# Keys times values in 64x64 quadrants with two permuting products, in a linear attention followed by a highway layer

## The chip, the core and the metric

The kernel runs on one core of a Trainium2 chip. The core has five engines that run side by side, each with its own queue of instructions: TensorE (PE, matrix products; its weight loads are listed apart as PEld), VectorE (DVE), ScalarE (ACT), GpSimd (POOL) and SyncE (SP, which here only issues transfers). Sixteen transfer engines (DMA) move data between the main memory and the on-chip memory. Products land in a separate accumulator memory, PSUM. The metric is the device time of one execution in microseconds (us).

## What is computed

Eight batches, eight heads, 576 tokens, 64 dims a head. Each head's queries go through a softmax over their dims, its keys through a softmax over the tokens; the keys and values of a head make a 64x64 matrix, and the queries are multiplied with it. The result, 4608 tokens by 512, goes through a highway layer with two 512x512 weights.

```python
def _attn_ref(q, k, v):                       # (8, 8, 576, 64) each
    q_s = np.exp(q - np.max(q, axis=-1, keepdims=True))
    q_s = q_s / (np.sum(q_s, axis=-1, keepdims=True) + 1e-09)
    k_s = np.exp(k - np.max(k, axis=2, keepdims=True))
    k_s = k_s / (np.sum(k_s, axis=2, keepdims=True) + 1e-09)
    kv = np.einsum('bhsd,bhse->bhde', k_s, v)
    return np.einsum('bhsd,bhde->bhse', q_s, kv)

def _moe_ref(x, w_h, w_t, b_t):               # x: (4608, 512)
    H = np.maximum(x @ w_h, 0.0)
    T = 1.0 / (1.0 + np.exp(-(x @ w_t + b_t)))
    return T * H + (1.0 - T) * x
```

## The kernel before

The whole program is a list of steps written out by hand, ORDER (lines 17 to 55). A step such as `kv_3` or `xe_5:A` calls one small function with a batch, group or tile number, and a letter picks the engine where there is a choice (A for ACT, D for DVE, P for POOL). Each engine works off its instructions in the order in which the list issues them; waits between engines follow from the data.

A batch b goes through these steps. `k`, `v` and `q` issue the loads on SP's queue, each buffer threefold. `ek` takes the exponential of the keys on ACT, `vc` casts the values to 16 bits, with a column of ones beside them. `kv` multiplies them on PE: for each head the 576 tokens lie as 9 slices of 64 partitions, and a product of one slice (64 tokens) takes 32 dims of one head, the even or the odd ones, as weights and 65 columns of values as the moving side. That is 8 heads x 9 slices x 2 halves = 144 products of 64x32 per batch, in tile positions (64 hh, 32 g). The 32 partitions of position g hold one half of the dims of a head, the other half lies in the same partitions at another place (m) of the free dimension. `kr` and `kn` on DVE take the reciprocal of the ones column's sums and scale the matrix into `kvb`. `eq` is the exponential of the queries on ACT, and `tr` turns them on DVE, two 16-bit dims as one 32-bit element; that is why the dims come in even and odd ones.

Then come 20 groups of tokens, `xu`, each of two tiles of 128 tokens (every fifth group is one tile, from the rest of two batches): PE multiplies turned queries and `kvb`, the two halves m = 0 and 1 added in PSUM. `kv` and `xu` share one PSUM buffer of four banks (pool ps_x, one buffer), so each waits until the one before has been read. `rs` and `x` on DVE divide by the sum and write x in 16 bits.

For each of 36 tiles: `xt` transposes x on PE, `xe` copies it out of PSUM, `bw` puts the bias in the gate's bank (a product with ones on PE, or a copy by ACT), `mt` and `mh` are the four products each with the two weights, `th` the tanh on ACT, `dd` the maximum on DVE, `gg`, `uu` and `oo` the rest on POOL or DVE, and `st` or `st1` the store. `wtc`, `whd` and `whc` prepare the weights once; `fill` issues idle products on PE at the start.

Lines that the prediction's steps touch: L222 `ek`, L227 `vc`, L243 `kv`, L250 `kr`, L253 `kn`, L260 `eq`, L278 `tr`, L291 and L301 `xu`, L313 `rs`, L319 `x`, L326 `xt`, L332 `xe`, L339 and L341 `bw`, L346 `mt`, L352 `mh`, L359 and L362 `th`, L366 `dd`, L155 `fill`.

Of the kernel before, what the change touches and what calls it, by code (L numbers as in the profile page):

```python
# [19 lines left out]
k_1_0_2 xe_1:D whc_0:A xu_1 whd_2:D whd_3:P whc_2:A mt_1_0 th_1_0 mt_0_0 rs_1 x_1 xt_2 ek_1_0_2 v_1_2_2 xe_2:D  # L20
vc_1_2_2:P mh_0 dd_0 mh_2 th_0_0 gg_0_0:P mh_1 bw_2_0 dd_2 bw_3_0:A gg_1_0:P dd_1 v_1_0_2 k_1_2_2 ek_1_2_2 q_1_0_8
eq_1_0_8 xt_3 xe_3:D mt_2_0 vc_1_0_2:D uu_0_0:P mh_3 q_1_8_10 dd_3 oo_0_0:D mt_3_0 tr_1_0_8 uu_1_0:P oo_1_0:P th_2_0
k_2_0_4 gg_2_0:P kv_1 kr_1 kn_1 eq_1_8_10 tr_1_8_8 v_2_0_4 bw_4_0 th_3_0 uu_2_0:P bw_5_0:A xu_2 rs_2 x_2 xt_4 xu_3
ek_2_0_4 tr_0_16_2 oo_2_0:P gg_3_0:P xe_4:D uu_3_0:P rs_3 tr_1_16_2 x_3 xt_5 mt_4_0 xe_5:A mh_5 q_2_0_18 v_3_0_4
k_3_0_4 th_4_0 vc_2_2_2:D vc_2_0_2:A q_3_0_18 xt_6 oo_3_0:P xu_4 rs_4 gg_4_0:P x_4 q_4_0_18 xe_6:A mt_5_0 mh_4 th_5_0
dd_5 dd_4 xt_8 xe_8:D eq_2_0_8 tr_2_0_8 kv_2 kr_2 kn_2 bw_8_0:A gg_5_0:P mt_8_0 eq_2_8_10 tr_2_8_8 mh_6 bw_6_0:A xt_7
# [20 lines left out]
eq_7_8_10 st_11 kv_7 oo_22_0:D kr_7 kn_7 uu_24_0:P mh_28 dd_23 dd_28 xt_29 mh_26 dd_26 xu_17 rs_17 xe_29:A xt_30
bw_29_0:A mt_29_0 x_17 bw_28_0:A oo_25_0:P mt_28_0 xe_30:A th_29_0 uu_23_0:P oo_24_0:P mh_27 oo_23_0:P st_10 tr_7_8_8
bw_27_0:A uu_26_0:P th_28_0:S uu_28_0:D xt_31 xe_31:A tr_7_16_2 dd_27 mt_27_0 bw_31_0:A th_27_0:S xt_32 xu_18
tr_6_16_2 rs_18 xe_32:A uu_27_0:D gg_29_0:P mt_31_0 x_18 oo_26_0:P th_31_0 mh_29 dd_29 mh_30 bw_30_0:A mt_30_0  # L50
oo_28_0:D bw_32_0:A st_13 oo_27_0:P st_12 uu_29_0:P gg_31_0:P dd_30 th_30_0:S xu_19 rs_19 oo_29_0:P uu_30_0:D
# [8 lines left out]
def kernel(  # L60
# [168 lines left out]
    def kv_of(b):  # L229
        return T[f"kvps{b}"][:, 0:2, 0:130].rearrange("p m (c e) -> p m c e", c=2)  # L230

    def kv(e, b):


# [1 line left out]
        for turn in range(2):
            for c in range(2):
                for j in range(NJ):
                    for g in range(4):
                        h = 4 * c + g  # L240
                        hh, i, m = h % 2, h // 2, (turn + h) % 2
                        rows, cols = slice(64 * hh, 64 * hh + 64), slice(32 * g, 32 * g + 32)
                        nc.tensor.matmul(  # L243
                            ps[cols, m, 65 * c:65 * c + 65], T[f"ek{b}"][rows, j, i, m:D:2],
                            v16[b % NV][rows, i, j, 0:65], start=(j == 0), stop=(j == NJ - 1),
                            skip_group_check=True, tile_position=(64 * hh, 32 * g))
# [34 lines left out]
    def xu(e, u):  # L281
        bs, J, its = groups[u]
        t = T[f"xu{u}"] = ps_x.tile([P, 4, DM], FP32, tag="xu", name=f"xu_{u}")
        if len(bs) == 1:
            for a in range(2):
                for c in range(2):
                    for m in range(2):
                        for g in range(4):
# [2 lines left out]
                            nc.tensor.matmul(  # L291
                                t[:, g, col:col + 65], turned_q(bs[0], c, m, 256 * J + P * a, P)(rows),
                                kvb[bs[0] % NKV][rows, m, c, 0:65], start=(m == 0), stop=(m == 1),
                                skip_group_check=True, tile_position=(32 * g, 0))
            return
        for c in range(2):
            for m in range(2):
                for w, b in enumerate(bs):
                    for g in range(4):
# [103 lines left out]
    def st1(e, i, h=0):  # L403
# [14 lines left out]
        wtc=wt_cast, whc=wh_cast, whd=wh_less_identity, ek=ek, vc=vc, kv=kv, kr=kr, kn=kn, eq=eq, tr=tr,  # L418
# [36 lines left out]
```

## Time and profile before

| | |
|---|---|
| median of 3 runs | 144.22 us (143.59 to 144.29) |
| the profiled execution | 142.23 us, its span 140.5 us |
| PE busy | 112.2 us (80% of the span), 2267 products |
| DVE busy | 98.2 us (70%) |
| ACT busy | 90.9 us (65%) |
| POOL busy | 85.9 us (61%) |
| moved by DMA | 40.17 MB, mean 286 GB/s |
| kv, L243 | 1152 products of 64x32, 12.5 us busy |
| xu, L291 and L301 | 640 products, 9.2 us busy |
| mt and mh, L346 and L352 | 292 products, 78.2 us busy |
| ek, L222 | 10 instructions, 17.4 us busy |

The span is the time from the first to the last instruction of one execution; 1.7 us lie around it. A line of the groups gives line, engine, operation, the program's names of what is written and read, shapes and count, then busy time and the mean of one instruction. Products of PE overlap, so the mean of one (197 ns in kv) is longer than the distance from one to the next. The chain of waits is followed back from the last instruction: at each step to what released it, or to the instruction before it; "issue" is time in which an engine waited for nothing that the profile shows. PEclk and "clock" are the share of full speed that TensorE's clock was granted.

### The profile page before, as it was taken

What the parts mean: (1) busy time and instruction counts of PE and PEld (TensorE: products, weight loads), DVE (VectorE), ACT (ScalarE), POOL (GpSimd) and SP (SyncE); (2) the same over time, 40 slices, a digit from 0 to 9 for tenths busy, and PEclk for the clock granted to TensorE, in tenths of its full rate; (3) what the DMA queues carried; (4) which work ended last, traced back from release to release, by engine and by line L of the source; (5) the groups of instructions that cost most, each with busy time, mean ns of one, the idle gap of its engine ahead of it and who ended that gap; (6) DMA issues with size and microseconds to landing.
All of it is one profiled execution on the core that took longest, in us unless ns stands there. A gap on an engine that the chain in (4) does not pass through costs nothing.

```text
span 140.5 us, 5171 instructions
## 1 busy us (share of the span) xinstructions
PE 112.2 (80%) x2267; PEld 58.9 (42%) x2267; DVE 98.2 (70%) x176; ACT 90.9 (65%) x121; POOL 85.9 (61%) x93
## 2 busy tenths in 40 slices
PE   6947879936997599189923999399999999999930
PEld 2315245524364255035522456145565464544510
DVE  3703786977477597557923498287999999998890
ACT  3345376776577595916931689349999978866710
POOL 0001546999139469494980437903998879989930
PEclk9997899996599999959995599869999999999996
DMA  4999999999999999999999999100291052724362
GB/s 138 261 398 407 401 392 387 394 395 398 392 396 410 394 387 392 403 402 405 396 401 399 404 396 355 40 0 0 82 398 53 5 201 103 296 84 167 132 269 106
DMA packets 14890, 40.17 MB, mean 286 GB/s; under 512 B 914, under 2 KB 1170, under 8 KB 14868
## 3 DMA queue, kind: packets, MB, share of 16 engines
q1 hardware_dynamic: 14576, 39.59, 73.9%
q8 instruction: 17, 0.28, 0.8%
q10 hardware_dynamic: 292, 0.27, 0.6%
q14 instruction: 5, 0.04, 0.1%
HBM read 30.41 MB, written 9.44 MB: 284 GB/s over the span
## 4 chain that ended last, share of the span: by engine, by line
PE 63%; DVE 13%; issue 10%; DMA 6%; ACT 3%; SPq 2%; DVEq 0%
PE tps L346 22%; PE gps L352 21%; PE turned L326 7%; PE kv L243 7%; DMA v<-in_v_dram 6%; PE xu L291 4%; DVE d L366 3%; DVE et L278 3%; DVE x L319 2%; ACT qe L260 2%; DVE o L392 2%; SPq L168 2%; DVE v L227 1%; PE turned L155 1%; DVE xT L332 1%
## 5 line engine op out<-in xcount | busy, mean ns | idle before, releaser
L392 POOL TENSOR_TENSOR o<-u,x 128x512 f32<-128x512 f16 (+1 forms) x30 | 35.6, 1195 | 7.4 <-DVE u L377 6.8
L346 PE MATMUL tps<-w16t,xT 128*128 128x512 f16 (+1 forms) x148 | 39.7, 403 | 0.2 <-DVE xT L332 0.2
L352 PE MATMUL gps<-w16h,xT 128*128 128x512 f16 x144 | 38.5, 400 | 0.0
L380 POOL TENSOR_TENSOR u<-g,d 128x512 f16<-128x512 f16 x23 | 27.7, 1212 | 4.7 <-DVE d L366 4.2
L366 DVE SCALAR_TENSOR_TENSOR d<-x,gps 128x512 f16<-128x512 f16 x36 | 24.3, 679 | 4.8 <-PE gps L352 4.7
L371 POOL TENSOR_SCALAR g<-th 128x512 f16<-128x512 f16 x23 | 14.1, 618 | 20.3 <-ACT th L362 20.3
L260 ACT ACTIVATE qe<-q 128x1024 f16<-128x1024 f32 (+1 forms) x16 | 18.6, 1164 | 6.3 <-DVE kvb L253 1.9
L319 DVE TENSOR_TENSOR x<-xu,rs 128x1024 f16<-128x1024 f32 (+1 forms) x20 | 22.2, 1112 | 0.3
L278 DVE STREAM_TRANSPOSE et<-qe 128x512 f32<-128x512 f32 (+1 forms) x24 | 20.0, 835 | 2.9 <-ACT qe L260 2.9
L243 PE MATMUL kv<-v,ek 64*32 64x65 f16 x1152 | 12.5, 197 | 10.3 <-issue 7.3
L346 PEld LDWEIGHTS <-xT 128*128 128x128 f16 x148 | 14.0, 104 | 15.0 <-issue 3.7
L352 PEld LDWEIGHTS <-xT 128*128 128x128 f16 x144 | 13.8, 102 | 14.7 <-issue 2.8
L222 ACT ACTIVATE ek<-k 128x2304 f16<-128x2304 f32 (+1 forms) x10 | 17.4, 1736 | 3.5 <-DMA k<-in_k_dram 3.5
L339 ACT COPY tps<-ball 128x512 f32<-128x512 f32 x29 | 16.8, 592 | 3.3 <-DVE d L366 3.1
L362 ACT ACTIVATE th<-tps 128x512 f16<-128x512 f32 x23 | 13.6, 596 | 8.1 <-PE tps L346 8.0
L332 ACT COPY xT<-turned 128x512 f16<-128x512 f16 x18 | 10.6, 586 | 12.8 <-PE turned L326 12.8
L326 PE MATMUL turned<-idh,x 128*128 128x128 f16 x144 | 15.0, 231 | 4.0 <-DVE x L319 3.3
L243 PEld LDWEIGHTS <-ek 64*32 64x32 f16 x1152 | 11.0, 94 | 13.1 <-issue 8.2
L326 PEld LDWEIGHTS <-x 128*128 128x128 f16 x144 | 10.6, 102 | 11.1 <-DVE x L319 4.1
L291 PE MATMUL xu<-kvb,et 32*128 32x65 f16 x512 | 7.8, 197 | 6.9 <-issue 5.1
L359 ACT ACTIVATE tps<-tps 128x512 f32<-128x512 f32 (+1 forms) x14 | 7.7, 550 | 5.8 <-PE tps L346 5.5
L291 PEld LDWEIGHTS <-et 32*128 32x128 f16 x512 | 5.5, 97 | 13.6 <-issue 7.3
(42 smaller groups left out, 82.3 us busy)
## 6 DMA issues: line engine op xcount, KB each, us to landing
out_dram<-o SPq DMA_DIRECT2D x16, 512.0 KB, 5.6
k<-in_k_dram SPq DMA_DIRECT2D x6, 1152.0 KB, 14.5
v<-in_v_dram SPq DMA_DIRECT2D x6, 1152.0 KB, 16.1
q<-in_q_dram SPq DMA_DIRECT2D x6, 1152.0 KB, 15.3
k<-in_k_dram SPq DMA_DIRECT2D x4, 576.0 KB, 9.1
q<-in_q_dram SPq DMA_DIRECT2D x2, 640.0 KB, 12.1
v<-in_v_dram SPq DMA_DIRECT2D x4, 288.0 KB, 4.1
v<-in_v_dram SPq DMA_DIRECT2D x2, 576.0 KB, 11.5
```

The source lines that it names most:

```text
L222: nc.scalar.activation(t[:, :, c:c + n].rearrange("p j c d -> p c j d"), src[:, c:c + n], AF.Exp)
L243: nc.tensor.matmul(ps[cols, m, 65 * c:65 * c + 65], T[f"ek{b}"][rows, j, i, m:D:2], v16[b % NV][rows, i, j, 0:65], start=(j == 0), stop=(j ...
L260: nc.scalar.activation(t[:, :, j * D:(j + n) * D], src[:, :, j * D:(j + n) * D], AF.Exp)
L278: nc.vector.transpose(dst, src)
L291: nc.tensor.matmul(t[:, g, col:col + 65], turned_q(bs[0], c, m, 256 * J + P * a, P)(rows), kvb[bs[0] % NKV][rows, m, c, 0:65], start=(m == ...
L319: nc.vector.tensor_mul(dst[:, :, 0:n], sums(u)[:, :, :, 0:64], T[f"rs{u}"][:, :, 0:n].unsqueeze(3).to_broadcast([P, 4, n, D]))
L326: nc.tensor.matmul(t[:, n], x_of(i)[:, n0 + n % 2:n0 + 2 * P:2], idh, is_transpose=True, start=True, stop=True, skip_group_check=True)
L346: nc.tensor.matmul(T[f"tps{i}_{h}"][:, cs], T[f"xT{i}"][:, n], w16["t"][:, n, cs], start=False, stop=(n == 3), skip_group_check=True)
L352: nc.tensor.matmul(t, T[f"xT{i}"][:, n], w16["h"][:, n], start=(n == 0), stop=(n == 3), skip_group_check=True)
L366: nc.vector.scalar_tensor_tensor(t, x_of(i), -0.5, T[f"gps{i}"], op0=ALU.mult, op1=ALU.max)
L380: nc.gpsimd.tensor_mul(t[:, cs], T[f"g{i}_{h}"][:, cs], T[f"d{i}"][:, cs])
L392: eng.tensor_add(t[:, cs], T[f"u{i}_{h}"][:, cs], x_of(i)[:, cs])
```

## The change

`kv` takes all 64 dims of a head as weights, so that a product is 64x64 and a batch has 72 of them, at four tile positions (64 hh, 64 (g // 2)). For this `ek` writes the 64 dims of a head's slice in another order, the 32 even ones first and then the 32 odd ones. The result has, per head, even dims in 32 partitions and odd dims in the 32 beside them, which is the place that `xu` needs for only half of the values. So `kp` moves the rest: two products with a 128x128 matrix of zeros and ones (`swap`, made once by `perm` on POOL) exchange neighbouring blocks of 32 partitions, and `kc` copies the result from PSUM to a new tile `kvm` (ACT; DVE for the last batch). `xu` takes a half from `kvb` or from `kvm` (`kv_rows`).

ORDER is written anew as a whole: batches come in the order 0, 1, 3, 2, 5, 4, 6, 7; 20 instead of 8 of the bias steps `bw` are products on PE; both `whc` move from ACT to DVE; the first load is now the first part of q. Of ORDER the diff below shows only the lines around the first batch and around batch 3.

```diff
 ORDER = """
-b_32 b_0 setupdve fill_10 bsplit v_0_3_1 bp fill_10 v_0_0_1 v_0_2_1 vc_0_0_1:A bc vc_0_3_1:D k_0_2_2 ek_0_2_2 k_0_0_2
-v_0_1_1 q_0_0_8 ek_0_0_2 vc_0_2_1:D bw_1_0 vc_0_1_1:D kv_0 w_t_0 wtc_0:P q_0_8_10 w_h_0 w_t_2 kr_0 eq_0_0_8 tr_0_0_8
-w_h_2 kn_0 fill_4 xu_0 rs_0 x_0 setuppool bw_0_0 fill_4 xt_0 whd_1:D eq_0_8_10 whd_0:P tr_0_8_8 xe_0:A xt_1 wtc_2:P
...
-mt_10_0 vc_3_2_2:P kv_3 dd_10 v_5_0_4 eq_3_0_8 tr_3_0_8 kr_3 oo_6_0:P gg_7_0:P uu_7_0:P eq_3_8_10 tr_3_16_2 bw_11_0:A
-kn_3 oo_7_0:P xt_11 xe_11:A tr_2_16_2 mh_9 gg_8_0:P uu_8_0:P th_10_0 gg_10_0:P tr_3_8_8 xu_7 bw_9_0:A oo_8_0:P
...
+q_0_0_8 b_0 setupdve fill_10 b_32 v_0_1_1 bsplit bp fill_12 bc v_0_3_1 setuppool v_0_2_1 vc_0_2_1:A vc_0_1_1:D k_0_0_2
+ek_0_0_2 perm bw_0_0 v_0_0_1 vc_0_0_1:P k_0_2_2 ek_0_2_2 w_t_2 wtc_2:P eq_0_0_8 vc_0_3_1:D kv_0 kr_0 kn_0 tr_0_0_8
+fill_4 kp_0 kc_0:A q_0_8_10 bw_2_0 xu_0 rs_0 x_0 fill_5 xt_1 eq_0_8_10 tr_0_8_8 bw_1_0 w_t_0 wtc_0:P w_h_0 xe_1:A
...
+gg_5_0:P mt_7_0 x_4 th_7_0 uu_5_0:P mh_4 mh_7 oo_3_0:P gg_4_0:P xe_6:D kv_3 gg_7_0:P oo_5_0:D mh_6 dd_4 k_2_0_4 dd_7
+xt_8 kr_3 kn_3 bw_6_0 uu_7_0:P oo_7_0:P dd_6 kp_3 ek_2_0_4 v_2_0_4 mt_6_0 kc_3:A vc_2_2_2:P tr_3_8_8 xe_8:A bw_8_0
+uu_4_0:P tr_3_16_2 vc_2_0_2:A th_6_0:S xu_7 rs_7 x_7 mt_8_0 th_8_0 mh_8 oo_4_0:P uu_6_0:D bw_13_0:A xt_13 xe_13:D
...
+    kvm = [consts.tile([P, 2, 66], FP16, name=f"kvm{i}") for i in range(NKV)]
+    swap = consts.tile([P, 2, P], FP16, name="swap")
...
+    def perm(e):
+        nc.gpsimd.memset(swap, 0.0)
+        for to in range(4):
+            r, w = 32 * (to ^ 1), to % 2
+            nc.gpsimd.tensor_copy(swap[r:r + 32, w, 32 * to:32 * to + 32], idh[r:r + 32, r:r + 32])
...
     def ek(e, b, c, n):
-        t = once(f"ek{b}", lambda: ekp.tile([P, NJ, 4, D], FP16, tag="ek", name=f"ek_{b}"))
-        src = T[f"k32{b}"].rearrange("p (c j d) -> p c j d", c=4, j=NJ)
-        nc.scalar.activation(t[:, :, c:c + n].rearrange("p j c d -> p c j d"), src[:, c:c + n], AF.Exp)
+        t = once(f"ek{b}", lambda: ekp.tile([P, 4 * NJ, D], FP16, tag="ek", name=f"ek_{b}"))
+        src = T[f"k32{b}"].rearrange("p (s r m) -> p s r m", s=4 * NJ, m=2)
+        dst = t.rearrange("p s (m r) -> p s r m", m=2)
+        at = slice(NJ * c, NJ * (c + n))
+        nc.scalar.activation(dst[:, at], src[:, at], AF.Exp)
...
-        for turn in range(2):
-            for c in range(2):
-                for j in range(NJ):
-                    for g in range(4):
-                        h = 4 * c + g
-                        hh, i, m = h % 2, h // 2, (turn + h) % 2
-                        rows, cols = slice(64 * hh, 64 * hh + 64), slice(32 * g, 32 * g + 32)
-                        nc.tensor.matmul(
-                            ps[cols, m, 65 * c:65 * c + 65], T[f"ek{b}"][rows, j, i, m:D:2],
-                            v16[b % NV][rows, i, j, 0:65], start=(j == 0), stop=(j == NJ - 1),
-                            skip_group_check=True, tile_position=(64 * hh, 32 * g))
+        for c in range(2):
+            for j in range(NJ):
+                for g in range(4):
+                    hh, i, col = g % 2, 2 * c + g // 2, 64 * (g // 2)
+                    rows = slice(64 * hh, 64 * hh + 64)
+                    nc.tensor.matmul(
+                        ps[col:col + 64, hh, 65 * c:65 * c + 65], T[f"ek{b}"][rows, NJ * i + j],
+                        v16[b % NV][rows, i, j, 0:65], start=(j == 0), stop=(j == NJ - 1),
+                        skip_group_check=True, tile_position=(64 * hh, col))
...
+    def kp(e, b):
+        for w in range(2):
+            nc.tensor.matmul(T[f"kvps{b}"][:, 2, 0:130].rearrange("p (c e) -> p c e", c=2), swap[:, w],
+                             kvb[b % NKV][:, w, :, 0:65], start=(w == 0), stop=(w == 1), skip_group_check=True)
+
+    def kc(e, b):
+        copy = nc.vector.tensor_copy if e == "D" else nc.scalar.copy
+        copy(kvm[b % NKV][:, :, 0:65], T[f"kvps{b}"][:, 2, 0:130].rearrange("p (c e) -> p c e", c=2))
+
+    def kv_rows(b, g, c, m):
+        rows = slice(32 * g, 32 * g + 32)
+        return kvb[b % NKV][rows, m, c, 0:65] if m == g % 2 else kvm[b % NKV][rows, c, 0:65]
...
-                                kvb[bs[0] % NKV][rows, m, c, 0:65], start=(m == 0), stop=(m == 1),
+                                kv_rows(bs[0], g, c, m), start=(m == 0), stop=(m == 1),
...
-                            kvb[b % NKV][rows, m, c, 0:65], start=(m == 0), stop=(m == 1),
+                            kv_rows(b, g, c, m), start=(m == 0), stop=(m == 1),
```

More of the change, by code (lines that the diff above doesn't have):

```diff
@@ L22 @@
[L22 to L26, printed above, removed]
@@ L47 @@
[L47 to L51, printed above, removed]
@@ new lines @@
+ek_0_0_2 perm bw_0_0 v_0_0_1 vc_0_0_1:P k_0_2_2 ek_0_2_2 w_t_2 wtc_2:P eq_0_0_8 vc_0_3_1:D kv_0 kr_0 kn_0 tr_0_0_8
+fill_4 kp_0 kc_0:A q_0_8_10 bw_2_0 xu_0 rs_0 x_0 fill_5 xt_1 eq_0_8_10 tr_0_8_8 bw_1_0 w_t_0 wtc_0:P w_h_0 xe_1:A
+whd_1:P xu_1 w_h_2 xt_0 rs_1 whd_2:P mt_1_0 th_1_0 xe_0:D mt_0_0 k_1_2_2 v_1_2_2 vc_1_2_2:P th_0_0 gg_0_0:P x_1 xt_2
+xe_2:A mt_2_0 ek_1_2_2 th_2_0 whd_0:D k_1_0_2 ek_1_0_2 whd_3:D whc_2:D tr_0_16_2 whc_0:D mh_2 dd_2 mh_1 mh_0 bw_3_0
+gg_2_0:P uu_2_0:P oo_2_0:P xt_3 dd_1 v_1_0_2 vc_1_0_2:A kv_1 dd_0 gg_1_0:P q_1_0_8 eq_1_0_8 xe_3:D kr_1 mh_3 q_1_8_10
@@ new lines @@
+uu_4_0:P tr_3_16_2 vc_2_0_2:A th_6_0:S xu_7 rs_7 x_7 mt_8_0 th_8_0 mh_8 oo_4_0:P uu_6_0:D bw_13_0:A xt_13 xe_13:D
+q_2_0_18 dd_8 gg_8_0:P uu_8_0:P kv_2 kr_2 xt_14 mh_13 kn_2 kp_2 mt_13_0 oo_8_0:P eq_2_8_10 xe_14:D tr_2_16_2 bw_14_0:A
+kc_2:A tr_2_8_8 xu_9 eq_2_0_8 rs_9 x_9 q_5_0_18 oo_6_0:P th_13_0 gg_13_0:P v_5_0_4 mt_14_0 dd_13 uu_13_0:P vc_5_2_2:P
+xu_6 rs_6 oo_13_0:P th_14_0:S eq_5_0_8 vc_5_0_2:P x_6 eq_5_8_10 mh_14 dd_14 xt_11 xu_8 tr_2_0_8 bw_11_0 xe_11:A
+k_5_0_4 xt_12 xe_12:A mt_11_0 th_11_0 rs_8 uu_14_0:D x_8 xt_17 xe_17:A mh_11 k_4_0_4 bw_17_0 gg_11_0:P bw_16_0
@@ new lines @@
+tr_5_0_8 xt_16 xe_16:D dd_11 oo_14_0:P xu_5 rs_5 v_4_0_4 mt_17_0 uu_11_0:P x_5 ek_5_0_4 th_17_0 bw_15_0:A mt_16_0
+th_16_0 gg_16_0:P xt_15 xe_15:D ek_4_0_4 mh_16 kv_5 mt_15_0 th_15_0 tr_5_8_8 xt_10 gg_17_0:P kr_5 kn_5 kp_5 kc_5:A
+gg_15_0:P mh_17 dd_16 xe_10:A oo_11_0:D q_4_0_18 st_1 v_6_0_4 bw_12_0 xu_12 dd_17 vc_4_0_2:A q_6_0_18 rs_12 uu_16_0:P
+k_6_0_4 mh_12 tr_5_16_2 x_12 mt_12_0 vc_4_2_2:A mh_15 th_12_0:S uu_17_0:P oo_17_0:P eq_4_0_8 dd_12 uu_12_0:D st_0
+dd_15 xt_23 kv_4 bw_23_0 mh_10 xe_23:A kr_4 kn_4 eq_4_8_10 xt_9 xe_9:A kp_4 oo_16_0:P kc_4:A mt_23_0 th_23_0 oo_12_0:P
@@ new lines @@
+uu_15_0:P gg_23_0:P vc_6_2_2:A bw_10_0 tr_4_0_8 xu_10 vc_6_0_2:P tr_4_8_8 st_2 mt_10_0 th_10_0 xt_22 mh_9 oo_15_0:P
+xe_22:A v_7_0_4 rs_10 x_10 dd_10 xu_13 xt_19 mh_23 dd_9 bw_22_0:A mt_22_0 rs_13 x_13 k_7_0_4 gg_10_0:P uu_10_0:P
+xe_19:A mh_19 dd_23 uu_23_0:P eq_6_8_10 tr_6_8_8 th_22_0 bw_9_0:A bw_19_0 q_7_0_18 xu_11 ek_6_0_4 rs_11 dd_19 xt_25
+xe_25:D mt_9_0 th_9_0:S mt_19_0 xt_18 th_19_0:S oo_23_0:P x_11 gg_22_0:P oo_10_0:P st_3 mh_22 kv_6 xe_18:A uu_9_0:D
+tr_4_16_2 eq_6_0_8 dd_22 xt_24 xe_24:A kr_6 uu_22_0:P oo_22_0:P uu_19_0:D mh_18 bw_18_0 bw_24_0:A xt_21 kn_6 kp_6
@@ new lines @@
+kc_6:A vc_7_2_2:A oo_9_0:D st1_17_0 xe_21:D dd_18 st_6 vc_7_0_2:P mt_18_0 xu_16 th_18_0 rs_16 mt_24_0 xt_20 x_16
+tr_6_0_8 st_7 gg_18_0:P bw_25_0:A uu_18_0:P mh_24 xu_14 rs_14 x_14 mt_25_0 st1_8_0 th_24_0 gg_24_0:P st_12 ek_7_0_4
+th_25_0 gg_25_0:P mh_25 st_8 dd_24 kv_7 mh_21 bw_20_0:A xe_20:D mt_20_0 dd_25 eq_7_0_8 tr_6_16_2 uu_24_0:P kr_7 kn_7
+kp_7 xt_29 bw_21_0:A mt_21_0 tr_7_0_8 kc_7:D xu_17 dd_21 eq_7_8_10 tr_7_16_2 oo_19_0:P mh_20 xe_29:A tr_7_8_8 th_20_0
+rs_17 x_17 th_21_0 oo_18_0:P st_10 mh_29 dd_29 uu_25_0:P gg_21_0:P xt_30 bw_29_0:A mt_29_0 xe_30:A xt_31 dd_20 xe_31:A
@@ new lines @@
+xu_18 oo_24_0:P uu_21_0:P bw_31_0:A oo_25_0:P st_5 mh_30 xt_32 th_29_0:S oo_21_0:P rs_18 x_18 uu_29_0:D dd_30
+gg_20_0:P uu_20_0:P mt_31_0 xe_32:A th_31_0 oo_20_0:P xu_15 st_13 rs_15 oo_29_0:D xt_26 st_11 mh_31 bw_30_0:A mt_30_0
+bw_32_0:A dd_31 mt_32_0 xe_26:A xt_33 th_30_0:S mh_32 x_15 uu_30_0:D gg_31_0:P uu_31_0:P oo_31_0:P dd_32 xe_33:A
+th_32_0:S xu_19 rs_19 uu_32_0:D oo_30_0:D xt_27 xe_27:A mh_26 bw_27_0:A bw_26_0 xt_28 xe_28:A dd_26 st_16 mt_26_0
+th_26_0:S x_19 uu_26_0:D oo_32_0:P st_17 mt_27_0 th_27_0 xt_34 xe_34:D gg_27_0:P mh_27 dd_27 mh_28 dd_28 oo_26_0:D
@@ L56 @@
+st1_26_0 bw_28_0:A mt_28_0 bw_33_0:A th_28_0:S xt_35 xe_35:A uu_27_0:P mt_33_0 uu_28_0:D mh_33 th_33_0 dd_33 mh_34
+bw_34_0:A mt_34_0 oo_28_0:D oo_27_0:P th_34_0:S mh_35 st_15 dd_34 bw_35_1 uu_34_0:D mt_35_1 th_35_1 gg_33_0:P
+uu_33_0:P oo_34_0:D bw_35_0 mt_35_0 th_35_0:S dd_35 uu_35_0:D oo_33_0:P st_18 gg_35_1:P uu_35_1:P oo_35_1:D st1_35_1:A
+oo_35_0:D st1_35_0:A
 """
@@ L229, in kv_of @@
     def kv_of(b):
[L230 removed]
+        return T[f"kvps{b}"][:, 0:2, 0:130].rearrange("p w (c e) -> p w c e", c=2)
     def kv(e, b):
         ps = T[f"kvps{b}"] = ps_x.tile([P, 4, DM], FP32, tag="xu", name=f"kv_{b}")
[L236 to L246 removed]
+        for c in range(2):
[7 more added lines that the diff above has]
+                        skip_group_check=True, tile_position=(64 * hh, col))
     def kr(e, b):
@@ L417 @@
         k=load_kv("k"), v=load_kv("v"), q=load_q, w=load_w, b=load_b, bp=bp, bc=bc,
-        wtc=wt_cast, whc=wh_cast, whd=wh_less_identity, ek=ek, vc=vc, kv=kv, kr=kr, kn=kn, eq=eq, tr=tr,
+        wtc=wt_cast, whc=wh_cast, whd=wh_less_identity, ek=ek, vc=vc, kv=kv, kr=kr, kn=kn, kp=kp, kc=kc, perm=perm, eq=eq, tr=tr,
         xu=xu, rs=rs, x=x, xt=xt, xe=xe, bw=bw, mt=mt, mh=mh, th=th, dd=dd, gg=gg, uu=uu, oo=oo, st=st, st1=st1)
```

27 lines of the change are left out of this document (3 added, 24 removed).

## The prediction

> **What bounds the kernel now.** I read the page first, then the chain of waits in order of time, then the stages of the span, and last the queue that carries instructions.
>
> ```profile
> PE   6947879936997599189923999399999999999930
> DVE  3703786977477597557923498287999999998890
> PEclk9997899996599999959995599869999999999996
> DMA  4999999999999999999999999100291052724362
> ```
>
> These are forty slices of 3.51 us. The transfer engines are full from slice 2 to slice 25, so all loads are in at about 25 x 3.51 = 87.8 us. TensorE (PE) is full only from slice 26. Until then it has holes, although loads run ahead of it, and PEclk drops to 5 behind them. The chain tells what they are (start, us, what):
>
> ```profile
> 44.56 0.23 PE xu L291 x16
> 44.79 2.43 issue
> ...
> 57.52 2.64 issue
> 60.16 0.30 PE xu L291 x8
> 60.46 3.17 PE tps L346 x8
> ...
> 69.89 1.24 PE kv L243 x139
> 71.13 4.72 issue
> 75.85 0.29 PE kv L243 x4
> ...
> 86.28 1.26 PE kv L243 x133
> 87.54 2.61 issue
> ```
>
> Four times PE stops in the middle of a run of equal small products, where no semaphore holds it: 2.43 + 2.64 + 4.72 + 2.61 = 12.4 us, all on the chain. Counted in the instruction order of the built program, the stops lie before PE's instructions 1473, 1985, 2498 and 3009, that is 512 apart.
>
> ```profile
> q8 instruction: 17, 0.28, 0.8%
> ```
>
> Queue q8 brought 17 packets of 0.28 MB / 17 = 16.5 KB; PE has 4546 instructions, 267 to a packet. Asked in stretches of 0.2 us, the DMA view has them at 15.6, 22.2, 31.2, 37.4, 44.8, 51.0, 57.6, 64.0, 73.2, 79.6, 87.6, 91.2, 101.8, 106.0, 110.6, 116.6 and 123.2 us. Laid against the order this is one packet per 256 instructions, with edges at 193 + 256k, and each packet comes when PE has just entered the block before it. At 41.55 us PE enters block 1217 and goes on past its end at 47.22 (5.7 us); 1729: 54.07 to 60.16 (6.1 us); 2241: 69.92 to 75.85 (5.9 us); 2753, with the transfers running out: 86.33 to 90.15 (3.8 us). So while the loads run, a block that PE works off in under 6.0 us makes it wait until 6.0 us are over, and later until about 3.8. A batch's kv (144 matmuls and 144 weight loads, 1.29 us) is more than a block: the four that stopped hold only 3.1, 2.2, 1.2 and 1.2 us of work.
>
> The stops cost again in clock (stage; busy time of PE, PEld, DVE, ACT, POOL; clock; DMA):
>
> ```profile
> 60.30:63.60 3.30, 3.30 (x19) 1.26 (x12) 1.93 (x3) 0.60 (x1) 2.75 (x3) 0.57 1.04 399
> 63.60:70.00 6.40, 6.40 (x125) 3.30 (x126) 5.71 (x11) 5.70 (x8) 4.89 (x6) 1.00 1.04 403
> 76.00:80.00 4.00, 4.00 (x17) 1.47 (x12) 2.13 (x4) 2.59 (x4) 0.83 (x2) 0.50 1.05 407
> 95.00:131.00 36.00, 36.00 (x693) 19.31 (x692) 33.43 (x56) 30.67 (x47) 31.50 (x31) 1.00 0.38 148
> ```
>
> After a stop the granted clock is about half: eight tps take 3.17 us instead of 1.73, and four take 1.71 instead of 0.86. Over the three stretches that is 1.4 + 2.0 + 1.8 = 5.2 us. From 95 to 131 us PE is 100% busy, DVE 93% and ACT 85%: with the holes gone, PE sets the pace and DVE follows closely.
>
> **The change part by part.** The sum starts from the profiled execution: 140.5 us span, 142.23 in all, so 1.7 around it. The runs' median, 144.22, is 2.0 above that.
>
> *Quadrants.* PE loses 1152 products and gains 576 of 64 columns of weights, plus 16 permuting ones: 3457 instructions instead of 4546. kv now costs 8.96 ns a product (1.29 us / 144). No 64x64 product is in the trace. The nearest rows are xu L301 (64 columns of weights, 32 in 0.27 us: 8.4 ns) and xu L291 (128 columns, 0.35 us: 10.9 ns). At worst a product costs as much as the two it replaces (17.9 ns: no gain); better than 8.4 is excluded, since no row of small products is much faster. I take 9.7, from the two nearest rows: 72 x 9.7 = 0.70 us, a gain of 8 x 0.59 = 4.7 us, bounds 0 and 5.5.
>
> *Permuting products.* Two kp per batch, each near the 55 ns of one xt transpose (four in 0.22 us): 8 x 0.11 = 0.9 us of PE. The copy kc of 130 columns is not in the trace. ACT rows of 512 and 1024 columns (586 and 1060 ns) make it about 0.24; bounds 0.1 and 0.41 (DVE's xT copy of 512): 7 on ACT 1.7 us, one on DVE. In the order mh, xt or mt stand between kv and kp (0.86 to 1.7 us against kr and kn, 0.7) and between kp and xu (0.86 to 1.1 us against kc, 0.35), so I cost this chain at nothing. Bare, it would be 0.5 us a batch. Behind a late kp stand all of PE's products; behind a late kc stand ACT's next xe, eq or th, for which PE, DVE and POOL wait.
>
> *Order.* Twelve more bias products are on PE instead of ACT copies: 12 x 0.216 = 2.6 us of PE, against 7.1 us off ACT. Three more fills lie in the wait for the first loads (PE sits 2.78 us before kv_0). On SP, q's first 512 KB go ahead of v and k: 0.52 MB at 397 GB/s put the last k of batch 0 back by 1.3 us. But eq_0 no longer comes behind kv_0, and xu_0 was held by fills and et until 15.4; I leave its start at 15.5 (1.3 us more if that is wrong). perm's five small POOL steps fill a POOL that waits 14.3 us for weights; without that cover they would cost under 1 us. The whc pair moves to DVE (2.1 us): behind x_1 (done near 21.0 us) come whd, whd, whc, et and whc, 0.29 + 0.29 + 1.0 + 0.3 + 1.0, so the three mh of tiles 0 to 2 run from 24.0 to 26.6 us, where before they ended at 24.2. The wait for x that follows (2.83 us before 32.88) takes that up, so I charge nothing; without it, up to 2.4 us. Of the casts of v, four leave DVE for POOL and ACT; by rows the work of DVE goes from 107.7 to 104.8 us and that of POOL from 88.4 to 92.0, neither above PE's pace. Three stores stand ahead of the last load on SP, as before. At the end one half tile goes by POOL, beside the other half: 0 to 0.5 us.
>
> *Blocks.* With the same rows as prices, the blocks of the new order from edge 193 hold 9.6, 3.5, 7.1, 5.5, 5.0, 6.8, 6.1, 5.5, 7.0, 6.2 and 5.1 us of PE work. The 3.5 is stretched beyond 5.8 by the start's waits for loads, and the 5.1 comes when 3.8 is enough. Against 6.0, three are short: 0.5 + 1.0 + 0.5 = 2.0 us remain of 12.4. If other waits stretch them it is 0; if blocks shift by one kv, up to 5.
>
> [...]
>
> *ek.* Its ACTIVATE now writes every second element 64 bytes away (even and odd dims apart); it wrote runs of 64. The 2304 columns took 2.12 us, 0.92 ns each. No ACT row writes that way. The nearest row that steps at each element is on another engine: DVE's et transpose, 1104 ns for 512 columns (2.16 ns). Bounds: 2.1 and 2304 x 2.16 = 5.0 us. All of ACT's own rows have its pace (qe 1.0 ns, ek 0.92), so I take 2.1 and keep 5.0 as a rival.
>
> [...]
>
> *Sum.* 140.5 - 12.4 + 2.0 (stops) - 5.2 (clock) - 4.7 (kv) + 0.9 (kp) + 2.6 (bias) = 123.7 us. Two floors lie under it. The last k lands one q (1.18 MB, 3.0 us) before 87.8, and ek_7 (2.1) makes it 87; from kv_7 on the new order has 26.6 us of PE work, and PE's last product lay 5.8 us before the end: 87 + 26.6 + 5.8 = 119.4. ACT's rows in the new order add to 91.4 us from its first ek on (8.6 us); at the 85.2% of 95 to 131 us, with 5.4 us after its last tanh: 8.6 + 107.3 + 5.4 = 121.3. Neither cuts the sum. 123.7 + 1.7 = 125.4 profiled; with the 2.0 of the median, 127.5 us.
>
> **The rivals.**
>
> *Longer link.* kv and xu share one PSUM buffer, and kr and kn wait in DVE's queue. If an x (1.2 us) stands ahead of them each time, kp, and with it every later product in PE's queue, waits 8 x 1.2 = 9.6 us: 137. For it: DVE is 93% busy when PE is full. Against it: before, PE waited for kvb only 1.7 us in all.
>
> *ek somewhat slower* (3.2 us, halfway by ratio): ACT 91.4 + 8 x 1.06 = 99.9 us, / 0.852 + 14.0 = 131.3 span, 135 us. The same evidence as the next.
>
> *Slower than before: ek at the transposes' rate.* At 5.0 us ACT has 91.4 + 8 x 2.85 = 114.2 us of work, at 85.2% 134.0, plus 14.0: 148.0 span, 152 us. It decides from an ek of 4.2 us at that share of ACT; if ACT as the bound reached 95%, from 5.7. For it: et. Against it: ACT's one pace over all its rows.
>
> *The change doesn't do what it says.* The stops stay at other places, since less PE work between edges brings each edge sooner: 140.5 - 4.7 + 0.9 + 2.6 = 139.3 span, 143.0 us. Against it: the block sums above.
>
> **How the numbers follow.** Forecast 0.65 (its own range 121 to 132), longer link 0.09, ek somewhat slower 0.09, stops stay 0.06, ek at 5.0 us 0.11. Range: from the floor (119.4 + 1.7 = 121) to just past the two middle rivals, 138.5, which leaves out less than 0.2. A measurement of this kernel tells 0.5% from no change. Faster: 0.65 + 0.09 + 0.09 and half of the stops, 0.86; same 0.03; slower 0.11.
>
> **What would show it.** Right: 13 packets or fewer on q8, "issue" under 4 us in the chain, no slice of PEclk at 5 between 45 and 95 us, kv near 10 ns a product, kv_7 near 91 us. Wrong: ek above 3 us; PE waiting for kvb or kvm; a stop behind blocks 961, 1217 or 1985; ACT full with holes in PE. Where ek stays at 2.1 us and the stops are gone, but the time is above 135, my sum has missed a wait.

## The result and the profile after

The changed kernel takes 194.37 us (median of 4 runs, 193.30 to 195.11) against 143.91 us before: a ratio of 1.350 (1.342 to 1.358). It is slower by 35%, where 127.5 us were forecast.

The forty slices of the changed kernel's page, now 4.81 us each:

```profile
PE   7801996536990370998508539993199129999970
ACT  2499439976299999878999996899969997676730
PEclk9975589657699575699955857999559966999996
DMA  5999999992980199649956901600005000424434
```

ACT, which was busy for 65% of the span, is now busy for 79%, more than any other engine. PE has more holes than before, and here and there the transfers stand still as well, although the loads are not yet done (slice 10, and slices 13 and 14): the buffers are full and wait for ACT. In all, the loads on SP's queue waited 28.4 us for ek and 19.3 us for the exponential of the queries to free a buffer. The groups of the changed kernel tell which instruction it is (busy time and mean of one | idle time before, and who ended it):

```profile
L235 ACT ACTIVATE ek<-k 128x2304 f16<-128x2304 f32 x6 | 63.0, 10496 | 0.0
L235 ACT ACTIVATE ek<-k 128x1152 f16<-128x1152 f32 x4 | 21.2, 5429 | 0.8 <-DMA k<-in_k_dram 0.8
L254 PE MATMUL kv<-v,ek 64*64 64x65 f16 x576 | 9.0, 230 | 36.3 <-ACT ek L235 32.5
```

One exponential of a batch's keys takes 10.5 us; it was 2.12. Together they are 84.2 us instead of 17.4, and PE stands 32.5 us before kv for them. It stands another 11.3 us before xu for kvm and 10.6 us before mh for th, whose steps on ACT (kc and th) come late. The instruction queue q8 brought 13 packets (0.21 MB), as the prediction had it for a program of 3457 instructions. The chain shows how the wait looks from elsewhere:

```profile
128.37 2.33 ACT ek L235
...
130.78 7.50 issue
138.29 1.46 ACT tps L384 x2
...
147.13 10.38 ACT ek L235
...
157.55 1.21 PE kv L254 x55
```

The 7.50 us of "issue" are not one of PE's stops of the kernel before. ACT's timeline has an ek from 128.31 for 10.47 us, and the next tanh and xe stand behind it in ACT's queue. PE's timeline shows what PE waits for in that time, namely the same ek, before kv:

```profile
138.83 1.21 PE L254 MATMUL kv<-v,ek 64*64 64x65 f16 x72 [7.10 <-ACT ek L235]
```

After kv it waits 0.28 us more for the xe. Further on the chain goes through a whole ek.

### The profile page after: what moved, and what is told of

Its sections match the earlier page's. It is cut to its first block, busy times and chain, and to the rows that moved or that the text cites. A ratio compares the mean times of both kernels' runs of the same rounds, so it can differ in the third digit from the quotient of the medians.

```text
span 192.4 us, 4081 instructions
## 1 busy us (share of the span) xinstructions
PE 122.0 (63%) x1722; PEld 61.0 (32%) x1722; DVE 96.3 (50%) x171; ACT 152.8 (79%) x120; POOL 89.6 (47%) x102
## 5 line engine op out<-in xcount | busy, mean ns | idle before, releaser
L235 ACT ACTIVATE ek<-k 128x2304 f16<-128x2304 f32 (+1 forms) x10 | 84.2, 8469 | 0.8 <-DMA k<-in_k_dram 0.8
L377 PE MATMUL gps<-w16h,xT 128*128 128x512 f16 x144 | 42.8, 432 | 10.7 <-ACT th L387 10.6
L396 POOL TENSOR_SCALAR g<-th 128x512 f16<-128x512 f16 (+1 forms) x25 | 15.8, 634 | 68.5 <-ACT th L387 58.6
L405 POOL TENSOR_TENSOR u<-g,d 128x512 f16<-128x512 f16 (+1 forms) x25 | 28.7, 1150 | 13.8 <-DVE rz L261 10.3
L417 POOL TENSOR_TENSOR o<-u,x 128x512 f32<-128x512 f16 x27 | 32.4, 1207 | 1.2 <-DVE u L402 0.3
L254 PE MATMUL kv<-v,ek 64*64 64x65 f16 x576 | 9.0, 230 | 36.3 <-ACT ek L235 32.5
L387 ACT ACTIVATE th<-tps 128x512 f16<-128x512 f32 (+1 forms) x25 | 16.3, 658 | 6.2 <-PE tps L371 5.7
L254 PEld LDWEIGHTS <-ek 64*64 64x64 f16 x576 | 8.0, 141 | 39.6 <-ACT ek L235 37.7
L316 PE MATMUL xu<-kvb,et 32*128 32x65 f16 x256 | 7.6, 202 | 11.9 <-ACT kvm L275 11.3
L338 DVE RECIPROCAL rs<-xu 128x16 f32<-128x16 f32 (+1 forms) x20 | 4.7, 234 | 17.5 <-PE xu L316 17.3
L402 DVE SCALAR_TENSOR_TENSOR u<-tps,d 128x512 f16<-128x512 f32 (+1 forms) x12 | 7.9, 655 | 10.6 <-ACT tps L384 10.4
## 6 DMA issues: line engine op xcount, KB each, us to landing
q<-in_q_dram SPq DMA_DIRECT2D x2, 640.0 KB, 12.6
```

Of the source, the lines that this page charges most:

```text
L235: nc.scalar.activation(dst[:, at], src[:, at], AF.Exp)
L254: nc.tensor.matmul(ps[col:col + 64, hh, 65 * c:65 * c + 65], T[f"ek{b}"][rows, NJ * i + j], v16[b % NV][rows, i, j, 0:65], start=(j == 0), ...
L377: nc.tensor.matmul(t, T[f"xT{i}"][:, n], w16["h"][:, n], start=(n == 0), stop=(n == 3), skip_group_check=True)
L387: nc.scalar.activation(t[:, cs], T[f"tps{i}_{h}"][:, cs], AF.Tanh, scale=0.5)
L405: nc.gpsimd.tensor_mul(t[:, cs], T[f"g{i}_{h}"][:, cs], T[f"d{i}"][:, cs])
L417: eng.tensor_add(t[:, cs], T[f"u{i}_{h}"][:, cs], x_of(i)[:, cs])
```

## The experiments

The theory after the result was that one thing alone is wrong: the pattern in which ek writes. The rivals were the longer link through kp and kc, the new order, and ek being slow only beside other work.

**1. The same values, read apart instead of written apart.** The exponential is walked in another order. The source is then read 8 bytes apart, and 32 elements in a row are written. What lands in memory is the same as in the changed kernel.

```diff
-        src = T[f"k32{b}"].rearrange("p (s r m) -> p s r m", s=4 * NJ, m=2)
-        dst = t.rearrange("p s (m r) -> p s r m", m=2)
+        src = T[f"k32{b}"].rearrange("p (s r m) -> p s m r", s=4 * NJ, m=2)
+        dst = t.rearrange("p s (m r) -> p s m r", m=2)
```

> The changed kernel with one line altered: ek walks through the halves in the other order, so that it reads the keys 8 bytes apart and writes runs of 32 (64 bytes); what is written is the same. Theory A (the write that changes its place at every element is what made ek 10.5 us, and nothing else slowed the kernel): ek about 2.1 us, ACT busy near 94 us, no PE wait on ek over 3 us, and the time near the 127.5 us of the prediction without it, 120 to 132. Rival B (the link kp and kc or the new order costs by itself): ek about 2.1 us, but still above 144 us, with waits on kvm or kvb. Rival C (a pattern with a step costs on the reading side too): ek stays above 4 us and the time above 150.

Measured: 122.68 us (121.95 to 124.44), a ratio to the kernel before of 0.852 (0.847 to 0.858). This version beats both kernels. Its slices (3.03 us each) and groups:

```profile
PE   6792877967599999879999999999994999999900
PEclk9999999999999999999999999999999999999998
```

```profile
L235 ACT ACTIVATE ek<-k 128x2304 f16<-128x2304 f32 x6 | 13.9, 2324 | 0.2 <-DMA k<-in_k_dram 0.2
L254 PE MATMUL kv<-v,ek 64*64 64x65 f16 x576 | 6.6, 193 | 3.7 <-ACT ek L235 1.5 <-ACT v L240 1.1 <-POOL v L240 1.0
```

ek is back at 2.3 us. PE is full from slice 12 (about 33 us) up to the end of the work but for slices 17, 18 and 31, and PEclk stays at 9 until the last slice. Rivals B and C fall: the time is well below 144 us, PE has no wait for kvm or kvb of 0.2 us or more, and reading apart costs 0.2 us an ek (2.32 against 2.12).

**2. The kernel before with only the writing changed.** Old products, old order; kv takes its 32 dims from the new places.

```diff
-        nc.scalar.activation(t[:, :, c:c + n].rearrange("p j c d -> p c j d"), src[:, c:c + n], AF.Exp)
+        src = T[f"k32{b}"].rearrange("p (s r m) -> p s r m", s=4 * NJ, m=2)
+        dst = t.rearrange("p j c d -> p (j c) d").rearrange("p s (m r) -> p s r m", m=2)
+        at = slice(NJ * c, NJ * (c + n))
+        nc.scalar.activation(dst[:, at], src[:, at], AF.Exp)
...
-                            ps[cols, m, 65 * c:65 * c + 65], T[f"ek{b}"][rows, j, i, m:D:2],
+                            ps[cols, m, 65 * c:65 * c + 65], T[f"ek{b}"].rearrange("p j c d -> p (j c) d")[rows, NJ * i + j, 32 * m:32 * m + 32],
```

> The kernel before, with ek alone writing even and odd dims 64 bytes apart (kv takes its 32 dims from the new place; old products, old order). Theory A: ek 10.5 us each and 84 us in all instead of 17.4, ACT near 158 us busy; the time goes to 185 to 210 us, so the whole loss and more sits in this one access pattern. Rival B: ek slow only beside the new order's other work (a port or buffer shared with it): ek under 5 us here, time under 160.

Measured in one run: 201.16 us. The group of ek:

```profile
L224 ACT ACTIVATE ek<-k 128x2304 f16<-128x2304 f32 (+1 forms) x10 | 84.1, 8458 | 1.8 <-DMA k<-in_k_dram 1.8
```

That is the same 84 us in a program that has the old products and the old order and neither kp nor kc. The pattern is slow by itself, and by itself it costs the old kernel some 58 us (201.16 against 143.50 for the kernel before, run beside it).

**3. Quadrants in the old order.** The kernel of the first experiment with the ORDER of the kernel before; `setuppool` and `perm` come early, each `kp` and `kc` after the product that follows `kn`, or before the next xu.

```diff
-b_32 b_0 setupdve fill_10 bsplit v_0_3_1 bp fill_10 v_0_0_1 v_0_2_1 vc_0_0_1:A bc vc_0_3_1:D
+b_32 b_0 setupdve fill_10 bsplit v_0_3_1 bp fill_10 v_0_0_1 v_0_2_1 vc_0_0_1:A bc setuppool perm vc_0_3_1:D
...
-kn_0 fill_4 xu_0
+kn_0 fill_4 kp_0 kc_0:A xu_0
```

> Quadrants, kp and kc with ek reading apart as in the first run, but in the order of the kernel before (kp and kc put behind the next product after kn, perm and its identity at the start). 3457 instructions less 12 bias products on PE; blocks of 256 instructions hold 5.1, 8.6, 5.1, 5.3, 6.1, 4.4, 9.8, 5.1 and 5.0 us of work from instruction 705 on. Theory of blocks (a block under 6.0 us makes PE wait while the loads run): stops of about 0.9 + 0.9 + 0.7 + 1.6 + 0.9 = 5 us or less, none over 2 us; time 126 to 134. If the new order is what counts: stops as long as before (over 2 us each) and above 138.

Measured: 131.56 us (median of four runs: one took 129.24, the others 131.50 to 131.93), where the runs of the kernel before beside it had a median of 143.50. So the quadrants alone bring 12 to 14 us. What PE waits for, from the list of waits (us in total, times, longest), in the kernel before and then here:

```profile
PE kv L243 <- issue: 7.3, 2, 4.7
PE xu L291 <- issue: 5.1, 2, 2.6
...
PE kv L273 <- DVE kvb L267: 5.9, 6, 2.1
...
PE xu L319 <- issue: 0.3, 1, 0.3
```

Of PE's stops 0.3 us is left, against 12.4 before and up to 5 expected. Why less is left than the theory of blocks wanted was not looked into; other waits can have stretched the short blocks. Line 273 is kp here: in the old order PE waits 5.9 us for kvb and 1.8 us for kvm. That is the longer link, and in this order it costs something.

**4. The price of a pattern.** Fourteen ACT exponentials of 512 columns at the end of the kernel before, with four copies on DVE and two on POOL behind them; two output buffers fewer make room.

```diff
+        exp(f16[:, 0:512], src)
+        exp(f16[:, 0:1024:2], src)
+        exp(f16[:, 0:2048:4], src)
+        exp(f16[:, 0:4096:8], src)
+        exp(f16[:, 0:512].rearrange("p (s m r) -> p s r m", s=8, m=2), apart)
+        exp(f16[:, 0:512].rearrange("p (m r) -> p r m", m=2), far)
+        exp(f16[:, 0:512].rearrange("p (m r e) -> p r m e", m=2, e=2), src.rearrange("p (r m e) -> p r m e", m=2, e=2))
...
+        exp(f16[:, 0:512].rearrange("p (s m r) -> p s m r", s=8, m=2), src.rearrange("p (s r m) -> p s m r", s=8, m=2))
...
+        exp(f32[:, 0:512].rearrange("p (m r) -> p r m", m=2), far)
```

> The kernel before with twenty instructions of 512 columns added at its end (four output buffers instead of six, to make room): ACT exponentials, DVE and POOL copies, each with another pattern of writing or reading. Its time as a whole says nothing. Theory A1 (each write outside the 16-byte line of the one before costs): on ACT contiguous about 0.5 us; steps of 4 and 8 bytes near that; steps of 16 bytes, and halves 64 or 512 bytes apart, near 512 x 4.56 = 2.3 us; runs of 8 elements in turn near 0.5 us; runs of 2 and 4 in between. A2 (what costs is a 2-byte write alone in its 4-byte word): runs of 2 back at 0.5 us, step of 4 bytes already 2.3 us, 32-bit writes 512 bytes apart 0.5 us. A3 (the pattern's inner length of two costs, on either side): the read apart with inner length 2 and contiguous write is slow as well. Reading 8 bytes apart with runs of 32: 0.5 us by all but rival C.

ACT's timeline at the end of that kernel (start, us), in the order of the lines above:

```profile
138.59 0.63 ACT L418 ACTIVATE f<-ball 128x512 f16<-128x512 f32 x1 [2.80 <-issue]
139.25 0.77 ACT L418 ACTIVATE f<-ball 128x512 f16<-128x512 f32 x1
140.05 1.34 ACT L418 ACTIVATE f<-ball 128x512 f16<-128x512 f32 x1
141.42 2.46 ACT L418 ACTIVATE f<-ball 128x512 f16<-128x512 f32 x1
143.91 2.47 ACT L418 ACTIVATE f<-ball 128x512 f16<-128x512 f32 x1
...
148.90 0.65 ACT L418 ACTIVATE f<-ball 128x512 f16<-128x512 f32 x1
...
150.91 0.65 ACT L418 ACTIVATE f<-ball 128x512 f16<-128x512 f32 x1
...
152.88 1.12 ACT L418 ACTIVATE f<-ball 128x512 f32<-128x512 f32 x1
```

Contiguous 0.63 us; steps of 4, 8 and 16 bytes 0.77, 1.34 and 2.46; halves 64 or 512 bytes apart 2.47 and 2.46; pairs of 16-bit elements 512 bytes apart 0.65; reading apart 0.65; 32-bit elements 512 bytes apart 1.12. None of the three theories holds as it stood. A1 wanted pairs in between and an 8-byte step near contiguous, A2 wanted the step of 4 bytes slow, and A3 falls with a read of inner length two and a contiguous write: 0.74 us (the line is not shown here).

**5. What the pattern costs, once more.** The 2304 columns of ek in a row took 2.12 us and 512 took 0.63: 0.83 ns for each further column. That leaves about 0.2 us fixed (0.63 less 512 x 0.83 ns). The step of 16 bytes cost as much as halves 512 bytes apart, 2.46 us, and the steps of 8 and 4 bytes about a half and a quarter of what lies above the 0.2 us. So the estimate from these times is a price for each write that goes on to another 16 bytes (another line, as it is called below): (2.46 - 0.2) / 512 = 4.4 ns. The steps of 8 and 4 bytes open 256 and 128 lines: 0.2 + 256 x 4.4 ns = 1.33 and 0.2 + 128 x 4.4 ns = 0.76, where 1.34 and 0.77 were measured. That made the theory for twelve more patterns:

```diff
+        exp(two(f16[:, 0:512], 64), pairs(src, 64))
+        exp(two(f16[:, 0:512], 32), pairs(src, 32))
...
+        exp(f16[:, 1:513].rearrange("p (m r e) -> p r m e", m=2, e=2), src.rearrange("p (r m e) -> p r m e", m=2, e=2))
+        exp(f16[:, 0:2048].rearrange("p (r x) -> p r x", x=8)[:, :, 0:2], src.rearrange("p (r x) -> p r x", x=2))
...
+        exp(two(f16[0:32, 0:512], 8), pairs(src[0:32], 8))
```

> The kernel before with twelve more ACT instructions of 512 columns at its end. In the first set of patterns 2-byte writes that change their 16-byte line each time took 2.46 us, pairs of them 0.65, steps of 8 and 4 bytes 1.34 and 0.77, and 4-byte writes 512 bytes apart 1.12. Theory F (ACT gathers writes within one 16-byte line; opening a line costs about 4.4 ns for a write that fills no 4-byte word, 1.8 ns for one that does): halves 8 bytes apart, in one line, near 0.6 to 0.7; 16, 32 and 64 bytes apart all 2.46; pairs from an odd element (half words) near 1.3 or above; pairs in steps of 16 and 32 bytes near 0.65; 4-byte halves 64 bytes apart 1.1, 8 bytes apart 0.65; copy as slow as exp (2.46); 32 partitions as slow as 128. Rival G (the cost is of the 4-byte word alone, whatever the line): 8 bytes apart as slow as 64. Rival H (it grows with the distance): 16 bytes apart well under 64 apart.

The same view of that kernel:

```profile
138.13 0.63 ACT L418 ACTIVATE f<-ball 128x512 f16<-128x512 f32 x1
138.79 2.47 ACT L418 ACTIVATE f<-ball 128x512 f16<-128x512 f32 x1
...
146.29 1.61 ACT L418 ACTIVATE f<-ball 128x512 f16<-128x512 f32 x1
147.94 0.66 ACT L418 ACTIVATE f<-ball 128x512 f16<-128x512 f32 x1
...
153.30 2.47 ACT L418 ACTIVATE f<-ball 32x512 f16<-32x512 f32 x1
```

Halves 8 bytes apart, within one line, are free (0.63), 16 bytes apart cost all (2.47, and 2.48 and 2.47 for 32 and 64). Pairs from an odd element, each across a 4-byte boundary, take 1.61, aligned pairs in steps of 16 bytes 0.66; 32 partitions are as slow as 128 (2.47 both). The 32-bit halves took 1.07 us at 128 bytes (the expectation says 64) and 0.63 at 8 bytes, and a copy 2.45. Theory F came out at each pattern; G and H fall. It is a fit to times: what happens inside was not looked at.

**6. Do the stops move with the edges?** The kernel before with 116 more PE instructions at its start.

```diff
-... bp fill_10 v_0_0_1 ...
+... bp edge_64 fill_4 v_0_0_1 ...
+    def edge(e, n):
+        for _ in range(n):
+            nc.tensor.matmul(spare[:, 0:1], blank[:, 0:P], blank[:, 0:1], start=True, stop=True, skip_group_check=True)
```

> The kernel before with 116 more PE instructions at its start (64 products of one column, six idle products of 512 columns less), nothing else: every edge of a 256-instruction block falls 116 instructions earlier in the work. Theory of blocks: the stops move with the edges. In place of the stops in xu_6, xu_7, kv_4 (after 139 products) and kv_5 (after 141), PE stops in kv_2 after about 114 products (block of 3.0 us of work, stop near 3), kv_3 after 118 (2.6, stop 3.4), kv_4 after 80 (3.6, stop 2.4), kv_5 after 83 (3.3, stop 2.7), perhaps in kv_1 after 131; each block with its stop near 6 us. Rival: the stops belong to certain products (the first xu after a kv, or kv's end): then they stay in xu_6, xu_7 and at the ends of kv_4 and kv_5. Time about that of before, 140 to 148.

Measured in one run: 143.31 us. Pieces of its chain, of kv_2 and kv_5:

```profile
47.37 1.03 PE kv L248 x110
48.41 2.90 issue
...
86.10 0.78 PE kv L248 x75
86.88 2.72 issue
```

By the timeline the stops fall after 131 products of kv_1 (2.99 us), 114 of kv_2, 118 of kv_3 (1.64 us), 81 of kv_4 (1.00 us) and 83 of kv_5. Three more of over 1 us I had not foreseen: one of 4.18 us at the end of kv_0, and two of 1.15 and 1.24 us in xu_15 and xu_17, after 105 us; counted along the order, they too lie at edges. None is left in xu_7 or at the ends of kv_4 and kv_5, nor in xu_5, which by the order is where the first stop of the kernel before lay (the expectation says xu_6). The places are those of the edges, which settles it against the rival. The sizes are less certain: 2.90 and 2.72 us in kv_2 and kv_5 are as expected, those in kv_3 and kv_4 are less than half of it.

**7. The new order with the old products.** The kernel before with the changed ORDER, without kp, kc and perm.

```diff
-b_32 b_0 setupdve fill_10 bsplit v_0_3_1 ...
+q_0_0_8 b_0 setupdve fill_10 b_32 v_0_1_1 ...
...
-... kn_3 bw_6_0 uu_7_0:P oo_7_0:P dd_6 kp_3 ek_2_0_4 v_2_0_4 mt_6_0 kc_3:A ...
+... kn_3 bw_6_0 uu_7_0:P oo_7_0:P dd_6 ek_2_0_4 v_2_0_4 mt_6_0 ...
```

> The new order with the old 64x32 products, without kp, kc and perm, and with the old ek. 3457 + 1152 - 32 instructions on PE; blocks from instruction 705 on hold 3.3, 7.1, 3.2, 3.3, 3.8, 7.8, 1.2, 5.9, 3.5 and 8.9 us of work. Theory of blocks: stops of 2.7, 2.8, 2.7, 2.2, 4.8 and 2.5 us, part of them under other waits; the order alone brings little, 134 to 145 us. Rival (the order is the gain, the quadrants only let it be written): below 131.

Measured: 144.52 us (ten runs), ratio 1.003 (0.998 to 1.008). The stops are back: PE's timeline has 2.64, 1.07, 1.72, 4.09, 1.57 and 1.47 us, in all 12.6 us where 17.7 were expected. Counted along the order, the first four lie at edges where a stop was expected, the last two at later ones, and two of the expected stops did not come. With the old products the new order is worth nothing; with the quadrants it is worth 7 to 9 us (129.24 to 131.56 in experiment 3, 122.68 in experiment 1). So the two parts of the change need each other.

**8. Two slow exponentials of eight.** The kernel of the first experiment, with ek of batches 2 and 5 writing apart.

```diff
+        walk = "p s r m" if b in (2, 5) else "p s m r"
-        src = T[f"k32{b}"].rearrange("p (s r m) -> p s m r", s=4 * NJ, m=2)
-        dst = t.rearrange("p s (m r) -> p s m r", m=2)
+        src = T[f"k32{b}"].rearrange(f"p (s r m) -> {walk}", s=4 * NJ, m=2)
+        dst = t.rearrange(f"p s (m r) -> {walk}", m=2)
```

> The first run's kernel, with ek of batches 2 and 5 writing apart again: ACT has 2 x 8.4 = 16.8 us more, a mean ek of 4.2 us, which is where the prediction's slower rival put the break-even with the kernel before. ACT as the bound at the 85.2% of that rival: 91.4 + 16.8 = 108.2 us, / 0.852 + 14.0 = 141.0 span, 143 us, as much as before. If each microsecond of a late ek is passed on whole: 122.7 + 16.8 = 139.5. If the buffers (three of keys, two of their exponentials) take up part of it: 128 to 135.

Measured: 142.58 us (ten runs), ratio to the kernel before 0.996 (0.991 to 1.002). The 16.8 us more of ACT became 19.9 us of time (142.58 - 122.68): nothing was taken up by the buffers. The two longest waits of PE are

```profile
PE xu L317 <- ACT kvm L276: 8.1, 1, 8.1
PE gps L378 <- ACT th L388: 7.9, 1, 7.9
```

By ACT's timeline each comes behind one of the two slow ek: kc starts at 49.70 us, behind the ek from 39.70, and th at 74.82, behind the ek from 64.85. So PE does not wait for the slow exponential itself, but for the short steps that stand behind it in ACT's queue. Two slow instructions undo all that the change brings.

## Why the prediction was wrong

**The step that failed** is the price of ek: "Bounds: 2.1 and 2304 x 2.16 = 5.0 us. All of ACT's own rows have its pace (qe 1.0 ns, ek 0.92), so I take 2.1". It measured 10.5 us, outside both bounds. None of ACT's rows wrote apart, so their common pace said nothing on this; and et, the row for the upper bound, is DVE's and moves 32-bit elements, where experiment 4 has 512 single 32-bit writes on ACT at 1.12 us and 512 single 16-bit ones at 2.46. What such writes take on ACT only experiments 4 and 5 showed: 0.63 us for 512 columns with halves 8 bytes apart, within one line, and 2.47 us from 16 bytes on. Two elements to a line are enough as an aligned pair, at 0.66 us; as single elements in steps of 8 bytes they still cost 1.34 us.

**The slower rival** had the mechanism for the changed kernel: ACT as the bound, at 85.2% of its time. There ACT is busy for 84% of the time from 8 to 187 us (150.3 of 179 us). At 10.5 us an ek the rival's formula gives (91.4 + 8 x 8.38) / 0.852 + 14.0 = 200.0 us of span; the kernel has 192.4. The price in it, 5.0 us, was half of the true one. Its break-even at a mean ek of 4.2 us came out in experiment 8, with 141.0 us of span computed and 140.7 measured, but that is partly luck: there ACT is busy for 81% of the time from 8 to 135 us, and the loss lies in PE's two long waits behind the slow ek, not in an ACT that is full throughout.

**The sum without ek** came close. It said 123.7 us of span and 125.4 for the profiled execution; experiment 1 has 121.1 and 122.9. Term by term, there:

- kv: 0.71 us a batch in the chain (0.70 said); kp 0.12 us (0.11); kc 0.27 us (0.24).
- Stops: one of PE is left, of 1.57 us (2.0 said), with 13 packets. That the size is near is luck. The prediction put its 2.0 us behind blocks 961, 1217 and 1985 (and then listed a stop there among its signs of being wrong); no stop of PE lies there. The one that came lies, counted along the order, at the end of block 2753, which the prediction let off because the loads would be over. They were not: PE enters that block at about 86.7 us with the transfers full up to slice 30 (91 us), and goes on past its end at 92.88, 6.2 us later. That the edges make the stops is shown by experiment 6. The price of about 6.0 us a block held there for kv_2 and kv_5, was too high for kv_3 and kv_4, and in experiment 3 hardly any of the stops came that it gives.
- The packets tell where the price comes from. In the kernel before, PE goes on 2.4 to 2.7 us after the packet at each of the four stops (44.8 to 47.22, 57.6 to 60.16, 73.2 to 75.85, 87.6 to 90.15). From entering the block to the packet it is 3.3 to 3.5 us at the first three, not "just entered", and 1.3 us at the fourth, where the transfers run out. So the whole difference between 6.0 and 3.8 us a block lies before the packet. At the stop of experiment 1 the packet comes between 90.2 and 90.6 us, 2.3 to 2.7 us before PE goes on.
- kv_7 starts at 86.67 us. The floor of loads and ek said 87, the list of signs near 91. So the measured span lies between that floor (119.4) and the sum (123.7).
- The sum is 2.6 us too high. It gave back only the half clock behind the stops after 45 us. The stretch near 35 us, where before four tps and four gps took 1.71 us each behind a wait of 2.83 us for x, is gone too: there the wait for x is 1.64 us and PEclk stays at 9. That this is the rest was only argued.

**The other rivals**: in experiment 1 the longer link did not show (PE waits 1.5 us for ek and 1.0 to 1.1 for v before kv, and no wait for kvm or kvb is listed). In the old order it did, with 5.9 and 1.8 us (experiment 3), and in the changed kernel kvm came 11.3 us late. So costing this chain at nothing was right for the new order with a short ek, and only there. The stops did not stay: 12.4 us of them became 1.57.

The changed kernel takes 71.7 us more than experiment 1 (194.37 - 122.68), and ek is busy for 65.3 us more (84.2 - 18.9). With PE's holes goes a slower clock as well: 0.796 of full was granted on average against 0.996, and mt and mh are busy 84.4 us instead of 72.6. How the 71.7 us divide between the two was not measured.

## What to carry to other kernels

An instruction whose count and shape stay the same is not free when its access pattern changes: ek went from 2.12 to 10.5 us here, so where no row of the same engine shows the pattern, take its price as open upwards. One long instruction can also hold up the short steps behind it in its engine's queue, and other engines wait for those: with two ek of 10.5 us in ACT's queue, PE waited 8.1 us for kvm and 7.9 us for th (experiment 8). Where a pattern must be split, the other order of the loops, which writes runs and reads apart, is the first thing to look at: it took 2.32 us an ek here. A program of many small products has a second length beside its time, that of its instructions: for PE's 4546 queue q8 brought 17 packets (0.28 MB), for 3457 it brought 13 (0.21 MB). While the transfers were full here, PE stopped at the ends of stretches of 256 instructions that it worked off fast, in the worst cases until about 6 us were over (5.7 to 6.1 us at three stops of the kernel before), whichever products lay there (in experiment 6 the stops went with the edges, to 2.90 us in kv_2 and 2.72 us in kv_5); how long a stop lasts was not always foreseen. An order written by hand fits one instruction stream; here the same list was worth 7 to 9 us with one set of products and nothing with the other.

## What the runs showed of the hardware that was not expected

- ACT writing 16-bit results one by one, each to another 16 bytes than the one before: 2.46 to 2.48 us for 512 columns against 0.63 in a row (by the estimate of experiment 5, 4.4 ns an element against 0.83), the same for exponential and copy (2.47 and 2.45 us), for 32 and 128 partitions (2.47 us both), and for 16 to 512 bytes of distance (2.47 and 2.46 us). An aligned pair at each place is nearly free (0.65 and 0.66 us). Reading in such patterns is nearly free too: 0.65 and 0.74 us.
- In experiment 4 the same 16-bit copy with halves 64 bytes apart took DVE 1.40 us instead of 0.43, and POOL 2.45 instead of 0.80, once each (DVE's beside ACT's last instructions).
